# A gated linear recurrence with an erf network behind it, on one core: weights narrowed by an integer addition, checks moved from the scalar to the vector engine

## The chip, the cores and the metric

The kernel runs on one core of one Trainium2 chip. A core has a matrix engine (PE, which loads weights as PEld and multiplies), a vector engine (DVE), a scalar engine (ACT), GpSimd (POOL), and queues that start transfers (DMA; SP is the engine that issues most of them). Each engine works through its own list of instructions in order; semaphores hold one until another has done its part. The metric is the time of one execution on the device, in microseconds (us). Here the median of the runs is 747.3 us.

## The reference

Two blocks follow each other. The first is a recurrence with a complex gate: for every batch, head and step t, a state S of 48 x 48 is turned and shrunk by the gate a, takes up the outer product of k and v, and is read by q. The second is a dense network with two weight matrices.

```python
# batch 4, heads 8, steps 768, head dim 48; tokens 3072, model 384, hidden 2048
mag = sqrt(a_re**2 + a_im**2)
scale = minimum(mag, 0.999) / (mag + 1e-6)
a_re_n, a_im_n = a_re * scale, a_im * scale
for t in range(S):
    S_re, S_im = ar*S_re - ai*S_im + outer(k[t], v[t]), ar*S_im + ai*S_re
    y[t] = q[t] @ S_re
# x: (tokens, 384), the heads side by side
h = x @ w_in                                   # 384 -> 2048
sp = maximum(h, 0) + log1p(exp(-abs(h)))       # softplus
out = (h * erf(sp)) @ w_out                    # 2048 -> 384
```

q, k, v and the gates are 4-byte floats. The weights arrive as 8-byte floats, 12.6 MB of them, and the kernel has to make 4-byte floats of them itself.

## The kernel before

The tokens are worked off in 12 units of 256 (`u`), each of two chunks of 128 (`c`). For each chunk the gates give an angle (arctan of a_im / a_re, summed over time by a product with a triangle of ones) and a decay (logarithms, summed likewise). Keys and queries are scaled and turned by them (`prep`), transposed by PE (`cols`), multiplied with each other (`scores`), and give the chunk's output `y` and the state for the next chunk (`state`). Then `ff_in` multiplies with w_in, `softplus` and `erf_times_h` apply the nonlinearity, and `ff_out` multiplies with w_out. A table of places, `WHEN`, says when each step is put among the others.

This way of computing is only right if the gates and weights lie in certain ranges, for instance |a_im| < a_re. So the kernel collects measures of them in the tiles `seen` while it runs, and at its end compares them with limits; if one is out of range, a slower path recomputes everything. The parts that the change touches are these.

Narrowing. The 8 bytes of a weight are two words, `lo` and `hi`. The weights come in 16 pieces of 128 x 768, eight of w_in (128 x 3 x 256) and eight of w_out:

```python
def seek(words, i):                       # how many weights are too close to zero
    hi = words.bitcast(FP)...[:, :, 1]
    act(out=hi, in_=hi, func=AF.Square)
    act(out=hi, in_=hi, func=AF.Exp, scale=-1e10, accum_out=zeros[:, i:i + 1])

def begin():
    ...
    ins = nc.scalar.mul(out=b, in_=lo, mul=2.0**-52)                              # ACT
    nc.vector.tensor_scalar(out=a, in0=hi, 0x07FFFFFF, 3, and, shift_left)        # DVE
    nc.vector.scalar_tensor_tensor(out=u, in0=hi, 0xC0000000, in1=a, and, or)     # DVE, into the weights
    nc.vector.tensor_scalar(out=a, in0=u, scalar1=0xFF800000, and)                # DVE, sign and exponent alone

def end():
    f, b, a = T["parts", i]
    nc.vector.tensor_tensor(out=b, in0=b, in1=a, op=OP.mult)                      # DVE
    nc.vector.tensor_tensor(out=f, in0=f, in1=b, op=OP.add)                       # DVE

# each piece: get (transfer), use (begin and end), again (a second transfer, later), look (seek on it)
```

(The arguments are shortened here.) The high word is cut to a 4-byte float with the last three bits of its mantissa at zero, and the low word is added as a float of the right size. The second transfer of each piece, between the fifth and the last unit, serves the check alone; the last two pieces are looked at in halves, so there are 18 looks.

Gates, per unit or, in the first two units, per chunk:

```python
def g_mag(u, cc=ALL):
    act(out=s, in_=ar, func=AF.Square, accum_out=large[:, i:i + 1])
    act(out=y, in_=ai, func=AF.Square)
    nc.vector.tensor_tensor(out=s, in0=s, in1=y, op=OP.add)

def g_off(u, cc=ALL):                     # is |a_im| < a_re everywhere?
    act(out=m, in_=ai, func=AF.Abs)
    nc.vector.tensor_tensor(out=m, in0=m, in1=ar, op=OP.subtract)
    act(out=m, in_=m, func=AF.Relu, bias=LEAST, accum_out=off[:, i:i + 1])

def g_tan(u, cc=ALL):
    act(out=th, in_=ar, func=AF.Ln)
    act(out=th, in_=th, func=AF.Exp, scale=-1.0)
    nc.vector.tensor_tensor(out=th, in0=th, in1=ai, op=OP.mult)     # a_im / a_re
```

The first steps of the program. `warm` issues products that nothing reads:

```python
WARM = (12, 9, 8, 4, 6)
def warm(n, t):
    for _ in range(n):
        tc.keep_in_program_order(nc.tensor.matmul(out=ps[:, 0:P], lhsT=t[:, 0:P], rhs=t[:, 0:P], start=True, stop=True))
...
warm(WARM[0], cold)
...
for c in range(C):
    g_tan(0, one[c]); g_mag(0, one[c]); warm(WARM[1 + c], T["th", 0][:, c])
... # logarithms, arctan, angle and decay of the first chunk
warm(WARM[3], T["th", 0][:, 1])
g_sin(0, c0)
for f in first[:2]: f()                   # prep of k and q, first chunk
g_angle(0, 1)
warm(WARM[4], T["th", 0][:, 1])
g_sin(0, c1)
...
for cc in one: g_off(0, cc)
```

A transposed query tile is copied out of PSUM by ACT in the first units (`u < WHEN["qact"]`, which is 3), later by DVE.

Of the kernel before, what the change touches and what calls it, by code (L numbers as in the profile page):

```python
# [10 lines left out]
FP = mybir.dt.float32  # L11
U8 = mybir.dt.uint8
I32 = mybir.dt.int32
U32 = mybir.dt.uint32
# [15 lines left out]

LEAST = 2.0**-30

# [4 lines left out]
def weave(*streams):  # L37
# [5 lines left out]
    for _, _, _, step in sorted(order, key=lambda e: e[:3]):  # L43
# [3 lines left out]

WHEN = {'qact': 3,
 'a00': [0.385, 0.377, 0.405, 0.415, 0.427, 0.308, 0.569, 0.485, 0.567, 0.63],
 'a01': [0.562, 0.528, 0.613, 0.636, 0.651, 0.625, 0.661, 0.663, 0.673, 0.683],  # L50
 'n': [0.676, 0.782, 0.769, 0.929, 1.105, 1.183, 1.312, 1.472, 1.61, 1.914, 1.96, 2.143, 2.151, 2.284, 2.395],
 'g1': [0.657, 0.707, 0.747, 0.758, 0.79, 0.797, 0.829],
 'att': {1: [[0.95, 1.297], 1.089], 2: [[1.716, 2.126], 1.029], 3: [[3.038, 3.627], 1.205]},
 'gate': {2: [1.242, 1.292, 1.402, 1.421, 1.352, 1.472, 1.392], 3: [1.516, 1.614, 1.92, 2.114, 2.598, 2.232, 2.18]},
 'hps': {0: [[0.75, 0.876], [1.01, 1.45]],
         1: [[1.788, 2.0], [2.366, 2.708]],
         2: [[3.136, 3.566], [3.538, 3.85]],
         11: [[11.947, 12.305], [12.367, 12.72]]},
 'act': {0: [2.6, 2.924],
         1: [3.335, 3.7],  # L60
         2: [4.208, 4.46],
         3: [4.9, 5.2],
         4: [5.752, 6.098],
         10: [11.62, 11.97],
         11: [12.455, 12.8]},
 'ops': {0: [3.02, 3.377, 3.703],
         1: [3.679, 4.329, 4.479],
         2: [4.454, 4.8, 4.886],
         3: [5.38, 5.6, 6.213],
         10: [12.123, 12.388, 12.988],  # L70
         11: [13.11, 13.3, 14.0]},
 'T': 5.1,
 'gr': [-1.569, -1.419, -1.119, -0.953, -0.498, -0.129, -1.299],
 'st': [0.014, 0.03, 0.059, 0.09, 0.12, 0.15, 0.2, 0.25, 0.28, 0.388],
 'hr': [1.117, 1.488, 1.588, 1.938],
 'ar': [1.565, 1.95],
 'or': [2.163, 2.683, 3.173],
 'c1': 0.5,
 'er': 0.25,
 'ag': [5.424, 6.26, 7.239, 8.239, 9.239, 10.239, 11.21],  # L80
 'n1': 2,
 'rest': 12.3,
 'ok': 13.7,
 'al': [[11.0, 11.39], [11.319, 11.75]]}


WARM = (12, 9, 8, 4, 6)

# [510 lines left out]
def quotient_path(  # L599
# [74 lines left out]
    spans, off, large, exps, inverse, zeros = seen  # L674
    for t in (off, large, zeros):
        nc.vector.memset(t, 0.0)

# [69 lines left out]
    def narrow(i, dst, src, home):  # L747
# [6 lines left out]
        def seek(words, i):  # L754
            hi = words.bitcast(FP).rearrange("p (n w) -> p n w", w=2)[:, :, 1]
            act(out=hi, in_=hi, func=AF.Square)
            act(out=hi, in_=hi, func=AF.Exp, scale=-1e10, accum_out=zeros[:, i:i + 1])

# [6 lines left out]
        def begin():  # L765
            words = T["raw", i].bitcast(U32).rearrange("p (k n w) -> p k n w", k=k_, w=2)
            lo, hi = words[..., 0], words[..., 1]
            f, u = dst, dst.bitcast(U32)
            a, b = split(sp.tile([P, PARTS], U32, tag="S", name="word")[:, 0:N]), lo.bitcast(FP)
            ins = nc.scalar.mul(out=b, in_=lo, mul=2.0**-52)  # L770
            if i < 3:
                in_order(ins)
            ins = nc.vector.tensor_scalar(out=a, in0=hi, scalar1=0x07FFFFFF, scalar2=3, op0=OP.bitwise_and,
                                          op1=OP.logical_shift_left)
            if "hold" in T:
                tc.add_manual_dep(ins.ins, T["hold"].ins.name, order, reason="place among others")
            nc.vector.scalar_tensor_tensor(out=u, in0=hi, scalar=0xC0000000, in1=a, op0=OP.bitwise_and,
                                           op1=OP.bitwise_or)
            nc.vector.tensor_scalar(out=a, in0=u, scalar1=0xFF800000, scalar2=None, op0=OP.bitwise_and)
            T["parts", i] = f, b, a.bitcast(FP)  # L780

        def end():
            f, b, a = T["parts", i]
            nc.vector.tensor_tensor(out=b, in0=b, in1=a, op=OP.mult)
            nc.vector.tensor_tensor(out=f, in0=f, in1=b, op=OP.add)  # L785

# [76 lines left out]
    def gate(u, cc):  # L863
        return [T[nm, u][:, cc[0]:cc[1]].rearrange("p c h d -> p c (h d)") for nm in ("ar", "ai")]
# [10 lines left out]

    def g_off(u, cc=ALL):

        ar, ai = gate(u, cc)
        m = T["y"][:, cc[0]:cc[1]]
        i = u * C + cc[0]  # L880
        act(out=m, in_=ai, func=AF.Abs)
        nc.vector.tensor_tensor(out=m, in0=m, in1=ar, op=OP.subtract)
        act(out=m, in_=m, func=AF.Relu, bias=LEAST, accum_out=off[:, i:i + 1])

    def g_tan(u, cc=ALL):
        ar, ai = gate(u, cc)
        th = g_("th", u, cc)
        act(out=th, in_=ar, func=AF.Ln)
        act(out=th, in_=th, func=AF.Exp, scale=-1.0)
        nc.vector.tensor_tensor(out=th, in0=th, in1=ai, op=OP.mult)  # L890

    def g_log(u, cc=ALL):
# [70 lines left out]
    def chunk(u, c):  # L963
# [14 lines left out]
        def cols(nm, g):  # L978
            def f():
                ps = ps_a.tile([P, HG, P], FP, tag="a", name="tr")  # L980
                for j in range(HG):
                    nc.tensor.transpose(out=ps[0:D2, j, :], in_=st[nm][:, g * HG + j].rearrange("p u d -> p (u d)"),  # L982
                                        identity=ident)
                t = att2.tile([P, HG, P], FP, tag=f"{nm}T", name=f"{nm}T", bufs=2 if nm == "k" else 3)
                (nc.scalar.copy if nm == "k" or u < WHEN["qact"] else nc.vector.tensor_copy)(out=t[0:D2], in_=ps[0:D2])  # L985
                st[nm, g] = t
            return f
# [283 lines left out]
    g_decay(0, 1)  # L1271
    for cc in one:
        g_off(0, cc)

    plan = list(zip(WHEN["a00"][2:], first[2:])) + list(zip(WHEN["a01"], chunk(0, 1)))
    plan += [(0.60, partial(load_qkv, 1))] + [(0.605, wt[j][0]) for j in (6, 7)]
    plan += [(WHEN["n"][j - 1], wt[j][1]) for j in range(2, 16)]
# [9 lines left out]
    for c, b in enumerate((E0, E1)):  # L1287
        plan += [(b, partial(f, 1, one[c])) for f in (g_tan, g_mag, g_log, g_off)] + [(b + 0.03, partial(g_total, 1, c))]
    plan += [(dec, partial(g_decay, 1, c)) for c in range(C)] + [(S1 + 0.001, partial(load_gates, 2))]
# [4 lines left out]
    for u in range(NU):  # L1294
# [5 lines left out]
        if u > 1:  # L1300
            mag, log, turn, angle, decay, sin, get = WHEN["gate"].get(
                u, [u + x for x in WHEN["gr"]])
            plan += [(mag, partial(g_mag, u)), (mag, partial(g_off, u)), (log, partial(g_tan, u)), (log, partial(g_log, u))]
            plan += [(turn, partial(g_turn, u)), (sin, partial(g_sin, u))]
# [12 lines left out]
    def check():  # L1317

        n = len(seen)
        sums = const.tile([P, n], FP, name="sums")  # L1320
        for i, t in enumerate(seen):
            nc.vector.tensor_reduce(out=sums[:, i:i + 1], in_=t, axis=mybir.AxisListType.X, op=OP.add)
# [63 lines left out]
```

## Time and profile before

| | |
|---|---|
| median of the runs | 747.3 us (746.47 to 753.23) |
| span of the profiled execution | 749.0 us |
| mean granted clock of PE | 0.978 |
| bytes moved | 54.5 MB, mean 73 GB/s |
| chain of work that ended last | PE 45%, ACT 28%, DVE 18%, DMA 5%, no visible wait 2% |

The page has the busy time of each engine, then the span in 40 slices of 18.7 us, in which a digit is the busy share in tenths and PEclk the clock that PE was granted. A product in 4-byte floats stands as two records. The groups name the line, engine, operation, tiles and shape, then busy time and the mean of one instruction, then the idle time of its engine just before and what ended that. The records of matrix products overlap each other, so their mean says less than the distance from one to the next: eight products of the second network, 16 records, take 5.16 us back to back.

### The profile page before, as it was taken

Reading aid. Unit: us, or ns where it says so; the run is one execution under the profiler, and the core shown is the slowest. Engines: PE = TensorE matmul, PEld = TensorE weight load, DVE = VectorE, ACT = ScalarE, POOL = GpSimd, SP = SyncE. Lnnn points to the kernel's source line nnn. Section 1 sums busy time; section 2 is a strip of 40 time slices with the busy share of each in tenths; the row PEclk is TensorE's granted clock in tenths of the full one; section 3 lists DMA queues with packets and bytes.
Section 4 is the critical chain, followed back from the end, with each engine's and each line's share of the span. In section 5 each row is a group of like instructions: output and inputs, shape, how many; then the busy total and the mean of one; then the engine's idle time right before and its main releaser. Section 6 shows DMA issues by size and latency. Waiting matters only on the chain.

```text
span 749.0 us, 12674 instructions
## 1 busy us (share of the span) xinstructions
PE 715.4 (96%) x5018; PEld 608.9 (81%) x5018; DVE 586.0 (78%) x1011; ACT 618.4 (83%) x849; POOL 1.1 (0%) x8
## 2 busy tenths in 40 slices
PE   8898989989999999999999999999999999999996
PEld 6677778866677678898898899898889889899985
DVE  6779999597858698969959949949949957956663
ACT  8797685997989998999798798798798788697760
POOL 0000000000000000000000000000000000000000
PEclk9599899999999999999999999999999999999999
DMA  9963666311212030350530521522311410300000
GB/s 222 226 145 61 158 162 166 67 28 26 44 33 47 27 54 22 59 134 22 138 51 25 137 43 35 137 37 60 111 33 49 96 33 22 127 1 16 7 22 26
DMA packets 156012, 54.50 MB, mean 73 GB/s; under 512 B 142612, under 2 KB 145704, under 8 KB 155944
## 3 DMA queue, kind: packets, MB, share of 16 engines
q1 hardware_dynamic: 153864, 53.22, 30.4%
q8 instruction: 41, 0.67, 0.4%
q10 hardware_dynamic: 2080, 0.39, 0.3%
q14 instruction: 27, 0.22, 0.1%
HBM read 48.82 MB, written 4.75 MB: 72 GB/s over the span
## 4 chain that ended last, share of the span: by engine, by line
PE 45%; ACT 28%; DVE 18%; DMA 5%; issue 2%; SPq 0%; DVEq 0%
PE hps L1062 16%; PE ops L1160 8%; PE ops L1122 6%; ACT L707 5%; ACT z L708 5%; ACT yy L708 4%; PE y L1042 4%; PE kv L1005 3%; DVE z L1090 3%; DVE yy L1091 3%; PE sc L993 3%; DVE e L1092 3%; PE tr L982 3%; ACT e L708 2%; DVE h L1093 2%
## 5 line engine op out<-in xcount | busy, mean ns | idle before, releaser
L1062 PE MATMUL hps<-xT,w_in_sb 128*128 128x256 f32 x1152 | 273.6, 384 | 5.7 <-DVE w_in_sb L785 4.6
L1062 PEld LDWEIGHTS hps<-xT,w_in_sb 128*128 128x128 f32 x1152 | 214.1, 191 | 40.7 <-issue 4.7
L707 ACT ACT_TABLE_LOAD x77 | 98.8, 1283 | 3.3 <-issue 2.1
L1090 DVE TENSOR_TENSOR z<-z,yy 128x512 f32<-128x512 f32 x96 | 62.5, 683 | 34.5 <-ACT e L708 34.3
L708 ACT ACTIVATE e<-z 128x512 f32<-128x512 f32 x96 | 57.3, 626 | 31.8 <-DVE h L1093 31.4
L1122 PE MATMUL ops<-w_out_sb,h 128*128 128x384 f32 x224 | 78.9, 498 | 1.0 <-DVE h L1093 1.0
L1064 ACT COPY h<-hps 128x512 f32<-128x512 f32 x96 | 55.0, 576 | 27.2 <-PE hps L1062 27.1
L1160 PE MATMUL ops<-w_out_sb,h 128*128 128x192 f32 x384 | 70.1, 326 | 1.0 <-DVE o L1171 1.0
L1160 PEld LDWEIGHTS ops<-w_out_sb,h 128*128 128x128 f32 x384 | 63.6, 190 | 2.4 <-DVE o L1171 1.4
L1122 PEld LDWEIGHTS ops<-w_out_sb,h 128*128 128x128 f32 x224 | 42.3, 194 | 27.1 <-issue 1.9
L1091 DVE SCALAR_TENSOR_TENSOR yy<-z,yy 128x512 f32<-128x512 f32 x96 | 62.4, 682 | 0.2
L1092 DVE TENSOR_TENSOR e<-e,yy 128x512 f32<-128x512 f32 x96 | 62.4, 682 | 0.1
L1093 DVE SCALAR_TENSOR_TENSOR h<-e,h 128x512 f32<-128x512 f32 x96 | 62.4, 682 | 0.1
L993 PE MATMUL sc<-qT,kT 96*128 96x128 f32 x384 | 52.5, 286 | 0.2 <-DVE qT L985 0.2
L993 PEld LDWEIGHTS sc<-qT,kT 96*128 96x128 f32 x384 | 49.4, 199 | 3.0 <-DVE qT L985 0.9
L1042 PE MATMUL y<-A,v 128*32 128x128 f32 x768 | 48.3, 281 | 1.9 <-ACT pr L708 1.1
L708 ACT ACTIVATE z<-h 128x2048 f32<-128x2048 f32 x24 | 45.9, 1911 | 4.3 <-DVE yy L1091 4.2
L1160 PE MATMUL ops<-T,S 128*128 128x192 f32 x256 | 48.0, 331 | 0.0
L708 ACT ACTIVATE yy<-z 128x2048 f32<-128x2048 f32 x24 | 45.9, 1912 | 0.4
L708 ACT ACTIVATE z<-z 128x2048 f32<-128x2048 f32 x24 | 45.9, 1913 | 0.3
L708 ACT ACTIVATE yy<-yy 128x2048 f32<-128x2048 f32 x24 | 45.9, 1911 | 0.3
L1160 PEld LDWEIGHTS ops<-T,S 128*128 128x128 f32 x256 | 43.2, 194 | 2.3 <-DVE S L1107 0.2
(107 smaller groups left out, 1128.9 us busy)
## 6 DMA issues: line engine op xcount, KB each, us to landing
raw<-in_moe_w_in_dram SPq DMA_DIRECT2D x8, 768.0 KB
raw<-in_moe_w_out_dram SPq DMA_DIRECT2D x8, 768.0 KB, 4.2
again<-in_moe_w_in_dram SPq DMA_DIRECT2D x8, 768.0 KB, 4.8
ar<-in_a_re_dram SPq DMA_DIRECT2D x24, 192.0 KB, 3.1
k<-in_k_dram SPq DMA_DIRECT2D x24, 192.0 KB, 4.0
q<-in_q_dram SPq DMA_DIRECT2D x24, 192.0 KB, 3.7
v<-in_v_dram SPq DMA_DIRECT2D x48, 96.0 KB, 3.3
out_dram<-o SPq DMA_DIRECT2D x24, 192.0 KB, 1.9
```

The costliest lines, as they stand in the source:

```text
L707: in_order(nc.scalar.preload_act_table_set(sets[0]))
L708: in_order(nc.scalar.activation(func=func, **kw))
L993: nc.tensor.matmul(out=ps[:, j, :], lhsT=st["k", g][0:D2, j, :], rhs=st["q", g][0:D2, j, :], start=True, stop=True)
L1042: nc.tensor.matmul(out=ps[b * QUAD:(b + 1) * QUAD, i, :], lhsT=lhsT, rhs=rhs, start=start, stop=stop)
L1062: nc.tensor.matmul(out=ps[:, e, :], lhsT=w_in_sb[:, kd, f0:f0 + P], rhs=T["xT", u][:, kd, :], start=(kd == 0), stop=(kd == KD - 1))
L1064: nc.scalar.copy(out=T["h", u, sl][:, i:i + 2, :], in_=ps)
L1090: nc.vector.tensor_tensor(out=z, in0=z, in1=y, op=OP.mult)
L1091: nc.vector.scalar_tensor_tensor(out=y, in0=z, scalar=-2.0, in1=y, op0=OP.add, op1=OP.mult)
L1092: nc.vector.tensor_tensor(out=e, in0=e, in1=y, op=OP.mult)
L1093: nc.vector.scalar_tensor_tensor(out=h, in0=e, scalar=1.0 / RT2, in1=h, op0=OP.add, op1=OP.mult)
L1122: nc.tensor.matmul(out=ps, lhsT=lhsT, rhs=w_out_sb[:, i, :], start=i == HALF, stop=i == KF - 1)
L1160: ins = nc.tensor.matmul(out=ps, lhsT=a(sl)[:, i], rhs=b(sl, i), start=sl == 0 and i == 0, stop=sl == NSL - 1 and i == HALF - 1)
```

## The change

It has five parts. A weight is narrowed by adding integers: ACT makes of the low word its upper three bits, rounded, and DVE adds them to the cut high word, so that a carry runs from the mantissa into the exponent by itself; this spares the mask and the multiplication. The checks of weights and angles are done by single reductions of DVE (the least absolute high word; the greatest absolute a_im / a_re) in place of chains on ACT. More unread products are issued at first. The query copies of the third unit move from ACT to DVE. And the places were fitted anew. What it is for: less work on ACT and DVE, and a PE that is not left idle in the first steps.

The core of the diff; most changed places in `WHEN` are cut:

```diff
-WARM = (12, 9, 8, 4, 6)
+WARM = (12, 9, 8, 8, 13, 5)
-WHEN = {'qact': 3,
+WHEN = {'qact': 2,
... (places of steps changed: some by a few hundredths of a unit; 'al', the last looks, by 0.15)
+ 'qone': 0}

         def seek(words, i):
             hi = words.bitcast(FP).rearrange("p (n w) -> p n w", w=2)[:, :, 1]
-            act(out=hi, in_=hi, func=AF.Square)
-            act(out=hi, in_=hi, func=AF.Exp, scale=-1e10, accum_out=zeros[:, i:i + 1])
+            nc.vector.tensor_reduce(out=zeros[:, i:i + 1], in_=hi, axis=mybir.AxisListType.X, op=OP.min,
+                                    apply_absolute_value=True)
...
-            ins = nc.scalar.mul(out=b, in_=lo, mul=2.0**-52)
+            ins = nc.scalar.mul(out=lo, in_=lo, mul=2.0**-29)
...
-            nc.vector.scalar_tensor_tensor(out=u, in0=hi, scalar=0xC0000000, in1=a, op0=OP.bitwise_and,
+            nc.vector.scalar_tensor_tensor(out=a, in0=hi, scalar=0xC0000000, in1=a, op0=OP.bitwise_and,
                                            op1=OP.bitwise_or)
-            nc.vector.tensor_scalar(out=a, in0=u, scalar1=0xFF800000, scalar2=None, op0=OP.bitwise_and)
...
         def end():
-            f, b, a = T["parts", i]
-            nc.vector.tensor_tensor(out=b, in0=b, in1=a, op=OP.mult)
-            nc.vector.tensor_tensor(out=f, in0=f, in1=b, op=OP.add)
+            a, lo = T["parts", i]
+            nc.vector.tensor_tensor(out=dst.bitcast(U32), in0=a, in1=lo, op=OP.add)
...
-    def g_off(u, cc=ALL):
-        ... (the three steps above)
     def g_tan(u, cc=ALL):
...
         nc.vector.tensor_tensor(out=th, in0=th, in1=ai, op=OP.mult)
+        i = u * C + cc[0]
+        nc.vector.tensor_reduce(out=off[:, i:i + 1], in_=th, axis=mybir.AxisListType.XY, op=OP.max,
+                                apply_absolute_value=True)
...
+    plan += [(0.40, partial(warm, WARM[5], T["th", 0][:, 1]))]
...
     def check():
+        nc.vector.tensor_scalar(out=off, in0=off, scalar1=-1.0, scalar2=0.0, op0=OP.add, op1=OP.max)
+        nc.vector.tensor_scalar(out=zeros, in0=zeros, scalar1=4e-5, scalar2=None, op0=OP.is_lt)
```

## The prediction

> **What bounds the kernel now.** I read the page's busy shares and slices first, then the windows view over stretches of 20 us and over single steps of the clock, then what PE waited for, and last the groups of the operations that the change touches. The share of busy time would end the matter at once:
>
> ```profile
> PE 715.4 (96%) x5018; PEld 608.9 (81%) x5018; DVE 586.0 (78%) x1011; ACT 618.4 (83%) x849; POOL 1.1 (0%) x8
> PE   8898989989999999999999999999999999999996
> PEclk9599899999999999999999999999999999999999
> ```
>
> With PE at 96% an engine that sheds other work seems to win nothing. But the clock's second slice is a 5, so part of PE's busy time is slow work. The windows view (time, then busy us of PE, PEld, DVE, ACT, POOL, then clock, DMA share, GB/s) shows where:
>
> ```profile
> 20.00:40.00 20.00, 17.86 (x117) 14.47 (x118) 14.15 (x23) 14.86 (x32) 0.00 (x0) 0.58 0.93 219
> 40.00:60.00 20.00, 18.38 (x135) 14.00 (x134) 17.31 (x32) 16.84 (x38) 0.00 (x0) 1.00 0.58 134
> 60.00:80.00 20.00, 16.33 (x90) 14.02 (x89) 19.90 (x29) 14.25 (x24) 0.00 (x0) 0.86 0.33 81
> 80.00:100.00 20.00, 17.99 (x203) 14.35 (x201) 17.75 (x30) 14.57 (x25) 0.00 (x0) 0.97 0.52 129
> 100.00:120.00 20.00, 18.94 (x162) 16.52 (x162) 18.35 (x30) 14.31 (x21) 0.00 (x0) 1.00 0.80 195
> 120.00:140.00 20.00, 20.00 (x159) 16.55 (x155) 18.97 (x28) 16.43 (x26) 0.00 (x0) 1.00 0.57 140
> 200.00:300.00 100.00, 99.11 (x610) 73.11 (x611) 78.56 (x137) 90.86 (x108) 0.00 (x0) 0.98 0.19 38
> ```
>
> From 200 us on PE is the bound: 0.9 us idle in 100. The first 140 us are another kernel: from 60 to 140 us DVE is busy 75 of 80 us, and PE idles 6.7 us and runs slow besides. A finer cut shows how the clock falls:
>
> ```profile
> 16.30:19.75 3.45, 1.43 (x13) 1.24 (x11) 3.00 (x5) 3.44 (x8) 0.00 (x0) 1.00 0.93 245
> 26.60:30.00 3.40, 3.40 (x20) 3.15 (x19) 0.21 (x1) 3.09 (x9) 0.00 (x0) 0.50 0.73 143
> 71.00:74.40 3.40, 1.03 (x10) 0.83 (x8) 3.40 (x5) 1.98 (x3) 0.00 (x0) 0.99 1.02 189
> 77.80:81.20 3.40, 3.40 (x9) 2.70 (x8) 3.40 (x6) 1.33 (x4) 0.00 (x0) 0.50 0.77 223
> ```
>
> Twice a stretch in which PE did 1.4 or 1.0 of 3.4 us is followed by half clock: from 19.75 to 36.8 us, and from 74.4 to 81.2 us. What PE waited for in those places, with total, times and longest:
>
> ```profile
> PE hps L1062 <- DVE w_in_sb L785: 4.6, 2, 3.5
> ...
> PE tr L982 <- DVE qt L974: 2.2, 1, 2.2
> PE tr L982 <- ACT qT L985: 2.0, 1, 2.0
> ```
>
> The 3.5 us wait is the one before 75.5 us, for a narrowed weight piece; the other two lie at 17.7 and 21.9 us.
>
> **What the Trainium skill says.** "TensorE: Matmul & The Clock Gate", section "What's actually happening": the slow clock is the default, a busy window of about 3.4 us releases it and an idle one brings it back. The trace agrees on the step (3.4 us) and the halving; it adds that a stretch 58% idle (16.30 to 19.75) is idle enough, and that coming back took 17 us the first time and 6.8 the second. "DVE: scalar operands, raw-bit mode, write accounting and state across instructions", section "Raw-bit mode": the DVE's adder is exact on bit patterns only below 2^24. So a 32-bit sum has to be made of halves; in the changed program's order of instructions the add does stand with elements of half a word (512 where the tile has 256). No run here has its time yet. "VectorE: DVE Perf Modes", section "The perf-mode tier table": tensor_reduce has only the 1x program. The one here is too small to tell (128x24 in 169 ns), so I price it as the 1x tensor_tensor of the same size.
>
> **The change part by part.** The groups (count, busy us, mean ns, idle before):
>
> ```profile
> L784 DVE TENSOR_TENSOR raw<-raw,word 128x768 f32<-128x768 f32 x16 | 15.3, 955 | 3.8 <-ACT raw L770 3.5
> L785 DVE TENSOR_TENSOR w_in_sb<-w_in_sb,raw 128x768 f32<-128x768 f32 x8 | 7.6, 949 | 0.0
> L779 DVE TENSOR_SCALAR word<-w_in_sb 128x768 uint32<-128x768 uint32 x8 | 7.6, 946 | 0.1
> L779 DVE TENSOR_SCALAR word<-w_out_sb 128x768 uint32<-128x768 uint32 x8 | 4.4, 555 | 0.1
> L703 ACT ACTIVATE again<-again 128x768 f32<-128x768 f32 x14 | 12.9, 920 | 5.1 <-DMA again<-in_moe_w_out_dram 4.2 <-DMA again<-in_moe_w_in_dram 0.9
> ```
>
> Narrowing, 16 pieces. L779 and L784 go, and L785 becomes the integer add. Removed: 0.95 + 0.95 = 1.90 us for each of 8 w_in pieces, 0.55 + 0.95 = 1.51 us for each of 8 w_out pieces, together 27.3 us. The add: if it takes a word in a cycle as L785 does, 0.95 us; I put 1.05 us, an estimate from that row with 0.1 us for being a program of its own, so 16 x 0.1 = 1.6 us come back. DVE: -25.7 us, all of it in the first 140 us, where DVE is the full engine.
>
> Checks of the weights. ACT loses 14 x (920 + 914) ns + 4 x (557 + 579) ns + 18 x 189 ns for reading the accumulator = 33.6 us, all after 300 us. DVE gains 14 x 0.95 + 4 x 0.56 = 15.5 us there, at 75 to 82% busy.
>
> Checks of the angles. For ten whole units ACT loses 842 + 838 + 191 ns, for four half ones 514 + 516 + 191 ns: 23.6 us. DVE loses one subtraction each (948 or 556 ns) and gains one reduction that I price the same: nothing.
>
> Query copies of unit 2 go from ACT to DVE (4 x 575 ns off ACT, 4 x 679 ns on to DVE). Unread products: 4 to 8, 6 to 13, and 5 new. At full clock 34 of their records took 4.18 us and a product has two, so one takes 0.25 us and 16 more take 3.9 us, laid into the idle stretches at 13.6, 17.7 and 21.9 us.
>
> Totals: ACT 618 to about 559 us, DVE 586 to about 578 us, PE the same work. Now to the path, stage by stage.
>
> 1. 17 to 40 us: 13 products fill some 2.9 us from 16.2 us on, so the stretch before 19.75 is no longer idle and the clock should stay up. From 26.6 to 33.4 us PE alone sets the pace (DVE is busy 0.21 us in one of those steps): its kv and score products take 6.2 us at half clock and would take 3.1. Transposes and the first y products (about 6 us of path in this stage) give another 2 us, and the first query copy, which now stands before two ACT steps (1.0 us) and after a removed Abs (0.5 us), gives 1 us. Sum -6 us.
> 2. 53 to 140 us: DVE sheds 13 pieces: 5 x 1.8 + 8 x 1.41 = 20 us. PE cannot follow all the way: its idle time there is 1.6 (50 to 60) + 3.7 + 2.0 + 1.1 = 8.4 us, and the second half-clock stretch costs half of 5.7 busy us = 2.8 us. Of these 11.2 us I take three quarters: -8.5 us.
> 3. 140 to 200 us: PE idles 3.5 us, ACT is at 91% and loses about 6 us of angle checks and copies: -1 us.
> 4. 200 to 730 us: PE idles 8.2 us and two short clock drops cost 3.4 us; some of that is ACT standing at the second load of weights (7.0 us of waits), but DVE will stand there now: -1.5 us.
> 5. Unread products that get in the way +1 us, two more small DVE steps in the closing check (137 to 169 ns each) +0.2 us.
>
> Sum: -6 - 8.5 - 1 - 1.5 + 1.2 = -15.8 us. 747.3 - 15.8 = 731.5 us, 2.1% less.
>
> **The rivals.** (a) PE is the bound and the shed work lay beside it. For: 96%, and 0.9 us idle per 100 after 200 us. Against: the slow clock and the waits at the start. It would give 743 to 747 us. (b) The integer add runs half a word per cycle: about 1.75 us, an estimate from twice L785's time less its start. Then DVE sheds 14.5 us instead of 25.7, stage 2 halves and the time is some 737 us. (c) The clock falls anyway, a step later (an idle stretch at 22 or 30 us): stage 1 gives 2 instead of 6, some 735 us. (d) DVE, now with the checks, stands before a late load and holds what PE wants after 400 us. Against: DVE is idle there a fifth of the time. It would add 3 to 5 us. (e) The relieved ACT (59 us) tightens stages 3 and 4 fully: down to 723 us.
>
> **Range and chances.** (a) to (d) are each less likely than not and mostly add, (e) stands against them; I take 723 to 741 us. The border of 2% is 732.4 us, just above my figure. Places that were fitted to this kernel speak for the gain to be realised; so faster by over 2% 0.55, within 2% 0.44, slower by over 2% 0.01.
>
> **What would show it.** Right: no half clock between 19.75 and 37 us nor near 75 us; the first hps product, at 45.2 us now, 5 to 8 us earlier; the wait of hps for w_in_sb below 1 us; the integer add at 1.0 to 1.2 us; the last narrowed piece, at 139.6 us now, before 125 us; ACT near 559 us and DVE near 578 us; from 200 us to the end nearly the same length. Wrong: a half-clock stretch of more than one step before 100 us, an add above 1.5 us, or more PE idle time after 300 us, behind DVE's reductions of the weights.

## The result and the profile after

The changed kernel takes 723.11 us in the median (722.15 to 725.71, 4 runs), the kernel before 748.12 us beside it (746.47 to 753.23): a ratio of 0.966, 95% interval 0.9605 to 0.9715. The profiled execution went from 749.0 to 720.6 us. The gain is 25 us, more than half as much again as the 15.8 us worked out. 723.1 us lies at the fast end of the stated 723 to 741 us; by the ratio, 747.3 x 0.966, it is 721.9 us, just beyond that end. The direction was right; two terms of the sum were too small.

The page after, busy shares first, then slices of 18 us:

```profile
PE 703.3 (98%) x5050; PEld 601.6 (83%) x5050; DVE 577.6 (80%) x1003; ACT 568.1 (79%) x749; POOL 1.1 (0%) x8
PE   8899999999999999999999999999999999999996
PEclk9999999999999999999999999999999999999999
```

ACT has shed 50 us (to 568; 559 us were predicted), DVE 8 us (578 predicted). The durations of ACT's records do sum to 59 us less, as worked out; but neighbouring records overlap, by some 0.09 us in the lines shown under e15, and busy time counts an overlap once, so 100 instructions fewer take 8 us of overlap with them. PE's busy time fell by 12 us though it does 16 more products: it has less slow time. The 5 in the clock's row is gone. The windows view of the changed kernel, the same stretches by the clock on the wall as were shown of the kernel before:

```profile
20.00:40.00 20.00, 18.72 (x209) 15.39 (x210) 16.52 (x32) 18.04 (x40) 0.00 (x0) 1.00 0.93 216
40.00:60.00 20.00, 19.88 (x106) 16.35 (x106) 12.97 (x22) 15.29 (x28) 0.00 (x0) 1.00 0.60 140
60.00:80.00 20.00, 20.00 (x172) 16.73 (x171) 19.55 (x30) 19.31 (x29) 0.00 (x0) 1.00 0.83 193
80.00:100.00 20.00, 18.81 (x179) 16.82 (x178) 19.71 (x33) 15.49 (x23) 0.00 (x0) 1.00 0.74 187
100.00:120.00 20.00, 20.00 (x202) 16.47 (x195) 16.22 (x24) 13.68 (x20) 0.00 (x0) 1.00 0.63 150
200.00:300.00 100.00, 99.53 (x645) 75.69 (x644) 90.42 (x157) 90.97 (x115) 0.00 (x0) 1.00 0.22 44
```

From 40 to 120 us PE is idle for 1.3 us in all. From 60 to 100 us DVE is as full as before (39.3 and 37.7 of 40 us), but with more of the work done by then. The groups of the changed operations (count, busy us, mean ns, idle before):

```profile
L782 DVE CUSTOM_DVE_ANT_0 w_in_sb<-raw,word 128x1536 uint16<-128x1536 uint16 x8 | 7.7, 958 | 5.7 <-PE hps L1053 4.2 <-ACT raw L769 1.4
L756 DVE TENSOR_REDUCE seen<-again 128x1 f32<-128x768 f32 x14 | 13.1, 945 | 2.7 <-DMA again<-in_moe_w_out_dram 1.8 <-DMA again<-in_moe_w_in_dram 0.7
L880 DVE TENSOR_REDUCE seen<-th 128x1 f32<-128x768 f32 x10 | 9.5, 949 | 0.1
```

The add costs 0.96 us where 1.05 us were put in, and it now waits for PE (4.2 us) where PE waited for it before. The reductions cost what the prediction took. All PE waits of one us or more that are left in the whole run:

```profile
PE tr L973 <- DVE kt L965: 2.1, 5, 0.9
PE sc L984 <- DVE qT L976: 1.3, 1, 1.3
PE tr L973 <- ACT kT L976: 1.3, 3, 0.8
PE unread L1210 <- DVE cold L665: 1.1, 1, 1.1
```

The wait of hps for w_in_sb, 4.6 us before, is gone. Of the other signs, these came true: the first hps product at 40.0 us instead of 45.2, the last narrowed piece at 116.8 us, no half clock before the closing steps. ACT's 559 us and the equal length from 200 us on did not.

**Where the time came from.** A stretch of the clock on the wall holds different work in the two kernels, so I lined them up by work. Each product that is read was given the distance at which products of its kind follow each other back to back; this sums to 663.5 us in every kernel here. A mark is the moment in the trace at which so much of this work is done.

| mark (us of work) | before | after | lead gained in the stage | predicted |
|---|---|---|---|---|
| 15 | 43.3 | 37.4 | -5.9 (stage 1) | -6 |
| 90 | 136.0 | 118.3 | -11.8 (stage 2) | -8.5 |
| 140 | 190.3 | 171.6 | -1.0 (stage 3) | -1 |
| 658 | 736.7 | 709.1 | -8.9 (stage 4) | -1.5 |
| end of the span | 749.0 | 720.6 | -0.8 (closing) | +1.2 |

The stages sum to the 28.4 us between the two spans, 3 us more than between the medians: the profiled execution of the kernel before took 750.8 us in all, 2.7 us above its median. The last stage can be read directly, since both windows hold the same 518 us of work. Before:

```profile
190.30:736.70 546.40, 537.03 (x3827) 468.62 (x3826) 429.82 (x750) 465.65 (x605) 0.00 (x0) 0.99 0.24 55
```

After:

```profile
171.60:709.10 537.50, 533.30 (x3830) 465.98 (x3829) 444.20 (x771) 423.57 (x528) 0.00 (x0) 1.00 0.24 57
```

PE's idle time fell from 9.4 to 4.2 us, and its busy time by 3.7 us with the same products, which is about half of the 6.8 us of half clock that only the kernel before had there. ACT went from 85% of the stretch to 79%, DVE from 79% to 83%.

### The profile page after: what moved, and what is told of

Its sections match the earlier page's. It is cut to its first block, busy times and chain, and to the rows that moved or that the text cites. A ratio compares the mean times of both kernels' runs of the same rounds, so it can differ in the third digit from the quotient of the medians.

```text
span 720.6 us, 12616 instructions
## 1 busy us (share of the span) xinstructions
PE 703.3 (98%) x5050; PEld 601.6 (83%) x5050; DVE 577.6 (80%) x1003; ACT 568.1 (79%) x749; POOL 1.1 (0%) x8
## 4 chain that ended last, share of the span: by engine, by line
PE 49%; ACT 25%; DVE 18%; DMA 5%; issue 3%; SPq 0%; ACTq 0%; DVEq 0%
PE hps L1053 19%; PE ops L1151 12%; ACT z L708 5%; ACT yy L708 5%; ACT L707 5%; PE sc L984 3%; PE y L1033 3%; PE tr L973 3%; DVE z L1081 3%; DVE yy L1082 3%; DVE e L1083 3%; PE kv L996 2%; DVE h L1084 2%; PE ops L1113 2%; DMA again<-in_moe_w_out_dram 2%
## 5 line engine op out<-in xcount | busy, mean ns | idle before, releaser
L1053 PE MATMUL hps<-xT,w_in_sb 128*128 128x256 f32 x1152 | 270.8, 381 | 1.3 <-ACT xT L1037 0.7
L708 ACT ACTIVATE e<-z 128x512 f32<-128x512 f32 x96 | 57.3, 626 | 37.2 <-DVE h L1084 36.8
L1113 PE MATMUL ops<-w_out_sb,h 128*128 128x384 f32 x224 | 76.6, 488 | 0.4 <-DVE h L1084 0.4
L984 PEld LDWEIGHTS sc<-qT,kT 96*128 96x128 f32 x384 | 47.9, 192 | 5.7 <-DVE qT L976 3.0
L984 PE MATMUL sc<-qT,kT 96*128 96x128 f32 x384 | 51.0, 278 | 1.7 <-DVE qT L976 1.3
```

What stands on the lines that cost most here:

```text
L708: in_order(nc.scalar.activation(func=func, **kw))
L984: nc.tensor.matmul(out=ps[:, j, :], lhsT=st["k", g][0:D2, j, :], rhs=st["q", g][0:D2, j, :], start=True, stop=True)
L1053: nc.tensor.matmul(out=ps[:, e, :], lhsT=w_in_sb[:, kd, f0:f0 + P], rhs=T["xT", u][:, kd, :], start=(kd == 0), stop=(kd == KD - 1))
L1113: nc.tensor.matmul(out=ps, lhsT=lhsT, rhs=w_out_sb[:, i, :], start=i == HALF, stop=i == KF - 1)
```

## The experiments

The change was taken apart into five parts: A, the check of the angles on DVE; L, the looks at the weights on DVE; N, the narrowing by an integer addition; U, the unread products; P, the places with the query copies of the third unit. Some kernels take one part out of the changed kernel, others put one or two into the kernel before. "Front" is the mark at 140 us of work, "late" the time from there to 658; both are of the one profiled execution. The median and the clock (mean granted clock of PE over a run, again the median) are of all runs; the clock of the kernel before is that of the 136 runs made beside the experiments.

| kernel | parts | median us | ratio to before, 95% | clock | front | late |
|---|---|---|---|---|---|---|
| before | none | 748.12 | 1 | 0.985 | 190.3 | 546.4 |
| e6 | N | 745.85 | 0.9971 (0.9948 to 0.9995) | 0.984 | 183.5 | 552.9 |
| e7 | U | 745.95 | 0.9964 (0.9941 to 0.9988) | 0.990 | 190.0 | 543.9 |
| e9 | P | 746.69 | 0.9997 (0.9971 to 1.0022) | 0.987 | 182.2 | 549.7 |
| e14 | N, P | 743.31 | 0.9949 (0.9918 to 0.9979) | 0.987 | 182.3 | 550.8 |
| e15 | A in the first two units | 744.51 | 0.9943 (0.9920 to 0.9965) | 0.983 | 182.8 | 546.5 |
| e16 | A in the other ten units | 745.42 | 0.9954 (0.9933 to 0.9975) | 0.987 | 189.0 | 542.4 |
| e10 | A | 738.87 | 0.9894 (0.9860 to 0.9928) | 0.992 | 185.9 | 542.2 |
| e11 | L | 744.31 | 0.9935 (0.9918 to 0.9953) | 0.986 | 190.6 | 540.4 |
| e12 | N, L | 741.47 | 0.9921 (0.9898 to 0.9945) | 0.986 | 189.5 | 542.6 |
| e13 | N, A | 736.94 | 0.9842 (0.9804 to 0.9880) | 0.992 | 178.5 | 545.1 |
| e17 | A, P | 735.23 | 0.9839 (0.9791 to 0.9886) | 0.995 | 177.8 | 542.3 |
| e4 | all but A | 738.01 | 0.9839 (0.9782 to 0.9896) | 0.990 | 181.4 | 542.1 |
| e3 | all but L | 728.54 | 0.9718 (0.9668 to 0.9769) | 0.998 | 171.6 | 543.5 |
| e8 | A, L | 736.49 | 0.9857 (0.9793 to 0.9921) | 0.988 | 183.0 | 537.1 |
| e5 | all but P | 730.49 | 0.9771 (0.9722 to 0.9821) | 0.998 | 176.8 | 539.8 |
| e2 | all but N | 728.76 | 0.9711 (0.9660 to 0.9761) | 0.998 | 179.4 | 536.5 |
| e1 | all but U | 725.40 | 0.9670 (0.9622 to 0.9718) | 0.993 | 174.0 | 539.5 |
| after | all | 723.11 | 0.9660 (0.9605 to 0.9715) | 0.998 | 171.6 | 537.5 |

The last column sorts itself largely by one thing: how many checks ACT still has in the later units. Two (the first six rows; e15 keeps both there): 543.9 to 552.9 us. One: 540.4 to 545.1. None: 536.5 to 539.8. Narrowing, places and unread products are in kernels of each kind and don't break this order, though the first two kinds overlap by a microsecond.

One profiled execution can lie away from its median: those of e6, e12, e14 and e10 are 4.8, 4.0, 3.1 and 2.7 us above theirs, that of e8 is 2.3 us below, so two or three us between two fronts or two late stages say little. Much of the spread is the clock: the 136 runs of the kernel before have clocks of 0.976 to 0.990 and times of 743.9 to 757.1 us, and a straight line through them gives 6.5 us for 0.01. At that rate the change's rise from 0.985 to 0.998 is worth some 8 of its 25 us, an estimate. Taken out of the changed kernel, only A (0.990) and U (0.993) let the clock fall; N, L and P leave it at 0.998.

### One part taken out of the changed kernel

**e1: the old numbers of unread products.**

```diff
-WARM = (12, 9, 8, 8, 13, 5)
+WARM = (12, 9, 8, 4, 6, 0)
```

> The changed kernel (723.1 us) with the old numbers of unread products, 4, 6 and none in place of 8, 13 and 5. Theory (they keep the clock up): a half-clock stretch of some 17 us comes back at about 20 us and the time is 728 to 731 us. Rival (the clock stays up because the relieved DVE and ACT feed PE sooner): no half clock in the first 100 us, 722 to 725 us.

725.40 us, 2.3 us more than the changed kernel; the ranges of the two overlap (724.91 to 726.91 here). The clock falls again, from 21.1 to 27.9 us and from 181.5 to 188.3 us, but for 6.8 us each. At 15 us of work the kernel is 1.4 us behind, and the clock of its runs is 0.993 instead of 0.998. The unread products do what they are for, but with the rest of the change in place it is worth little. Neither theory fits.

**e2: the old narrowing.**

```diff
-            ins = nc.scalar.mul(out=lo, in_=lo, mul=2.0**-29)
+            ins = nc.scalar.mul(out=b, in_=lo, mul=2.0**-52)
...
+            nc.vector.tensor_scalar(out=a, in0=u, scalar1=0xFF800000, scalar2=None, op0=OP.bitwise_and)
...
-            nc.vector.tensor_tensor(out=dst.bitcast(U32), in0=a, in1=lo, op=OP.add)
+            nc.vector.tensor_tensor(out=b, in0=b, in1=a, op=OP.mult)
+            nc.vector.tensor_tensor(out=f, in0=f, in1=b, op=OP.add)
```

> The changed kernel with the narrowing of before: DVE gets back two operations for each of 16 pieces, some 27 us, in the first 120 us. Theory (DVE is the bound of that stretch): the last piece lands 12 us later or more, the time is 732 to 737 us. Rival (other parts of the change had already freed DVE): below 727 us.

728.76 us, between the theories: the narrowing is worth 5.7 us in the median and 7.8 us at the front mark. The last piece is narrowed 18.6 us later. The loss lies wholly in front, as predicted, but is only part of the front's gain.

**e3: the looks back on ACT.**

```diff
-            nc.vector.tensor_reduce(out=zeros[:, i:i + 1], in_=hi, axis=mybir.AxisListType.X, op=OP.min,
-                                    apply_absolute_value=True)
+            act(out=hi, in_=hi, func=AF.Square)
+            act(out=hi, in_=hi, func=AF.Exp, scale=-1e10, accum_out=zeros[:, i:i + 1])
```

> The changed kernel with the check of the weights back on ACT: 33 us of ACT more after 300 us, 15 us of DVE less. Theory (the 10 us won after 140 us come from the relief of ACT): 727 to 731 us, with PE waiting for ACT's decay or copies again. Rival (they come from the new places): 722 to 725 us.

728.54 us, as the theory had it; the front is the same to a tenth of a microsecond, and the late stage 6.0 us longer. Here are the PE waits of e3 from 300 to 712 us:

```profile
PE kv L996 <- ACT pr L708: 2.6, 4, 1.1
PE tr L973 <- ACT kT L976: 1.7, 3, 0.9
PE ops L1151 <- DVE o L1162: 1.7, 1, 1.7
PE tr L973 <- DVE kt L965: 1.0, 1, 1.0
```

In the changed kernel the same view has two lines:

```profile
PE tr L973 <- DVE kt L965: 1.2, 4, 0.5
PE tr L973 <- ACT kT L976: 0.2, 1, 0.2
```

The looks themselves never appear as what PE waits for. What appears is `pr` and `kT`, short steps that come after a look in ACT's list: a look of two passes, with its wait for the second transfer (6.9 us of such waits in e3, 7.0 in the kernel before), holds them up. The kernel before shows the whole of it in the chain of work that ended last (start, length, what):

```profile
538.23 6.35 DMA again<-in_moe_w_out_dram
544.58 0.02 issue
544.60 0.91 ACT again L703
545.51 0.46 ACT h L1064
545.97 0.89 ACT again L708 x2
546.86 0.85 ACT pr L708 x3
547.71 0.04 issue
547.76 1.89 PE kv L1005 x16
```

The second transfer lands, the two passes of the look follow, then `pr`, and then the `kv` products, for which PE had stood idle for 1.2 us. In e3 all four waits for `pr` have a look just ahead in the same way. On DVE the same look holds up nothing that PE needs at once: ACT itself waits 4.9 us for looks in the changed kernel, and PE doesn't wait behind it. Of the 6.0 us that e3 loses late, 5.5 are idle time of PE. This is most of the missing late gain of 7.4 us (8.9 measured, 1.5 predicted).

**e4: the check of the angles back on ACT.**

```diff
+        act(out=m, in_=ai, func=AF.Abs)
+        nc.vector.tensor_tensor(out=m, in0=m, in1=ar, op=OP.subtract)
+        act(out=m, in_=m, func=AF.Relu, bias=LEAST, accum_out=off[:, i:i + 1])
...
-        nc.vector.tensor_reduce(out=off[:, i:i + 1], in_=th, axis=mybir.AxisListType.XY, op=OP.max,
-                                apply_absolute_value=True)
```

> The changed kernel with the check of the angles back on ACT as Abs, subtraction, Relu: 24 us of ACT more over the whole span, DVE the same. Theory (ACT's relief): 726 to 730 us, some 2 us of it in the first 60 us. Rival (the new places): 722 to 725 us.

738.01 us: 15 us more (13 by the ratios), beyond both theories, and the costliest part to lose. It is 9.8 us behind at the front mark and 4.6 us longer late. In its first 60 us the PE waits begin with

```profile
PE sum L915 <- ACT th L709: 3.2, 2, 2.9
PE tr L980 <- ACT qT L983: 1.8, 1, 1.8
```

Neither wait is there with more than 0.5 us in the changed kernel. (In this profiled execution a load of a_im for the first unit also landed 1.6 us late and put back all that follows; that much is not the edit's.)

**e5: the old places,** with the query copies of the third unit left on DVE.

```diff
- 'a01': [0.526, 0.422, 0.611, ...],
+ 'a01': [0.562, 0.528, 0.613, ...],
... (all other entries of WHEN likewise)
```

> The changed kernel with all places of before (the query copies of unit 2 stay on DVE). Theory (the moved and saved work makes the gain, the places only trim it): 727 to 733 us. Rival (most of the gain is the fitting): above 736 us.

730.49 us, as the theory had it: 5.2 us at the front mark, 2.3 us late.

### Parts put into the kernel before

**e6: N alone** (the lines of e2 the other way round).

```diff
-            nc.vector.tensor_tensor(out=b, in0=b, in1=a, op=OP.mult)
-            nc.vector.tensor_tensor(out=f, in0=f, in1=b, op=OP.add)
+            nc.vector.tensor_tensor(out=dst.bitcast(U32), in0=a, in1=lo, op=OP.add)
```

> The kernel before with the narrowing by an integer addition alone. Theory (DVE is the bound from 53 to 140 us and sheds 26 us): 736 to 741 us, the last piece at 128 us or earlier, no half clock near 75 us. Rival (PE cannot follow, or another wait takes over): above 744 us.

745.85 us (740.38 to 751.25, 20 runs), in the rival's range. Of the theory the last piece (at 125.5 us) and the missing half clock near 75 us came true, but not the time. At the front mark the kernel is 6.8 us ahead, close to the predicted 8.5, though part of that is the clock's (6.8 us of half clock there, 23.9 in the kernel before). Its late stage is 6.5 us longer:

```profile
183.50:736.40 552.90, 542.25 (x3828) 473.23 (x3827) 430.80 (x751) 466.40 (x606) 0.00 (x0) 0.98 0.23 55
```

PE is idle 10.7 us there (9.4 before), and its clock is halved for 17.0 us, at 191.2, 542.8, 600.8 and 652.0 us (6.8 us before, at 200.7 and 548.8). The Trainium skill, "TensorE: Matmul & The Clock Gate", section "HAM oscillation — how this bites in real kernels", prices such a stretch at half its length. That makes 8.5 against 3.4 us, an estimate, 5.1 more; the trace agrees with 5.2 more busy us for the same products. With 1.3 us of idle time this is the whole loss in this execution. But this execution took 750.67 us, 4.8 above the median, and the clock of all 20 runs, 0.984, is that of the kernel before: narrowing alone leaves the amount of half clock as it was. The PE waits from 150 us on begin with

```profile
PE kv L1002 <- ACT pr L708: 3.7, 5, 1.5
PE tr L979 <- ACT kT L982: 2.5, 3, 1.9
```

**e7: U alone.**

```diff
-WARM = (12, 9, 8, 4, 6)
+WARM = (12, 9, 8, 8, 13, 5)
+    plan += [(0.40, partial(warm, WARM[5], T["th", 0][:, 1]))]
```

> The kernel before with the new unread products alone (8, 13 and 5). Theory (they hold the clock up in the first 37 us): no half clock from 19.75 to 36.8 us, 742 to 745 us. Rival (the idle time near 30 us lets it fall anyway): 746 to 749 us.

745.95 us, between the two ranges. In the profiled execution the rival was right: the clock is halved from 25.3 to 39.0 us instead of 19.8 to 36.8. But the clock of that execution is 0.984. The median of the 20 runs is 0.990, and nine of them lie above 0.990, which none of the 136 runs of the kernel before does. So the unread products hold the clock up in part of the runs, and the gain of 0.36% fits that.

**e8: A and L together, all else old.**

```diff
-            act(out=hi, in_=hi, func=AF.Square)
-            act(out=hi, in_=hi, func=AF.Exp, scale=-1e10, accum_out=zeros[:, i:i + 1])
+            nc.vector.tensor_reduce(out=zeros[:, i:i + 1], in_=hi, ..., op=OP.min, apply_absolute_value=True)
...
-    def g_off(u, cc=ALL):
+        nc.vector.tensor_reduce(out=off[:, i:i + 1], in_=th, ..., op=OP.max, apply_absolute_value=True)
```

> The kernel before with both checks, of the weights and of the angles, on DVE; nothing else is changed. Theory (ACT's relief is worth 10 us after 140 us and some at the start): 735 to 740 us. Rival (without fitted places the relief lies beside the path): 744 to 748 us.

736.49 us: the two checks alone bring nearly half of the gain. In the profiled execution the late stage has the whole of its gain already, 537.1 us against 537.5 in the changed kernel:

```profile
183.00:720.10 537.10, 534.64 (x3828) 466.50 (x3827) 441.96 (x767) 422.80 (x525) 0.00 (x0) 1.00 0.24 56
```

**e9: P alone.**

```diff
-WHEN = {'qact': 3,
- 'a01': [0.562, 0.528, 0.613, ...],
+WHEN = {'qact': 2,
+ 'a01': [0.526, 0.422, 0.611, ...],
```

> The kernel before with nothing but the new places (and the query copies of unit 2 on DVE). Theory (the places are fitted to the shed work and are worth something only with it): 744 to 750 us, with the half clock before 37 us still there. Rival (the places are worth some 7 us by themselves, as they are when they are taken out of the changed kernel): 738 to 743 us.

746.69 us, no difference that can be measured, as the theory had it. Its profiled execution is ahead in front (with 6.8 us of half clock there) and longer late, like e6's.

**e10: A alone** (the angle lines of e8).

```diff
-    def g_off(u, cc=ALL):
+        nc.vector.tensor_reduce(out=off[:, i:i + 1], in_=th, ..., op=OP.max, apply_absolute_value=True)
```

> The kernel before with only the check of the angles moved to DVE. Theory (this check stood in the chain of the first units, where ACT's absolute value and relu sat before the steps that PE waits for, and it is the larger of the two checks): 738 to 742 us, ahead of before by 4 us or more when PE has done 60 us of its products. Rival (the two checks together give their 12 us only because ACT is relieved as a whole, each alone little): 743 to 747 us.

738.87 us, as the theory had it, the largest single part.

**e11: L alone** (the weight lines of e8).

```diff
-            act(out=hi, in_=hi, func=AF.Square)
-            act(out=hi, in_=hi, func=AF.Exp, scale=-1e10, accum_out=zeros[:, i:i + 1])
+            nc.vector.tensor_reduce(out=zeros[:, i:i + 1], in_=hi, ..., op=OP.min, apply_absolute_value=True)
```

> The kernel before with only the check of the weights moved to DVE. Theory (worth what taking it out of the changed kernel cost, some 4 to 5 us, all after 300 us, as PE no longer stands behind ACT's pr and kT): 742 to 745 us, no difference before 300 us. Rival (the place of the look matters little as long as ACT has the angles too): 746 to 749 us.

744.31 us, as the theory had it; the front is unchanged (190.6 us) and the late stage 6.0 us shorter, the same 6.0 that e3 lost.

**e12: N and L.**

```diff
+            nc.vector.tensor_reduce(out=zeros[:, i:i + 1], in_=hi, ..., op=OP.min, apply_absolute_value=True)
...
+            nc.vector.tensor_tensor(out=dst.bitcast(U32), in0=a, in1=lo, op=OP.add)
```

> The kernel before with the narrowing by an integer addition and the check of the weights on DVE, the rest as before. With the narrowing alone 8 us were gained in the first 100 us of products and lost again, most of it after 500 us. Theory (it is ACT, with its looks at the weights, that gives it back late): the gain is kept, 735 to 740 us. Rival (it is given back by the clock or by the places, whatever ACT does): 741 to 746 us.

741.47 us, inside the rival's range: 0.8% where N and L alone sum to 0.9%. So relieving ACT of the looks does not by itself keep the narrowing's lead. Its profiled execution, 4.0 us above the median of the 11 runs, drew the long stretch of half clock, 17.1 us from 23.6 us on, so that its front is no measure of the narrowing.

**e13: N and A.**

```diff
+        nc.vector.tensor_reduce(out=off[:, i:i + 1], in_=th, ..., op=OP.max, apply_absolute_value=True)
...
+            nc.vector.tensor_tensor(out=dst.bitcast(U32), in0=a, in1=lo, op=OP.add)
```

> The kernel before with the narrowing by an integer addition and the check of the angles on DVE, the rest as before. The narrowing alone gave 2 us, the angles alone 9. Theory (the lead of the narrowing is lost because PE runs up against ACT; with ACT relieved in every unit the lead is kept): 730 to 734 us. Rival (the two simply add, as narrowing and the check of the weights did): 735 to 739 us.

736.94 us, the rival's range: 1.6%, with 1.35% the sum of the two alone. The front's lead is 11.8 us, and from 28 us until the closing steps the clock doesn't fall.

**e14: N and P.**

```diff
-WHEN = {'qact': 3,
+WHEN = {'qact': 2,
...
+            nc.vector.tensor_tensor(out=dst.bitcast(U32), in0=a, in1=lo, op=OP.add)
```

> The kernel before with the narrowing by an integer addition and the new places, both checks still on ACT. Each alone gave 2 us or less. Theory (the places are fitted to the earlier weights and keep the lead): 735 to 740 us. Rival (with ACT loaded as before the lead goes, whatever the places): 742 to 747 us.

743.31 us, the rival's range. In the profiled execution the front is 8.0 us ahead and the late stage 4.4 us longer than before: with both checks on ACT half of that lead goes in spite of the new places.

**e15: A in the first two units alone.**

```diff
     def g_tan(u, cc=ALL):
+        if u < 2:
+            nc.vector.tensor_reduce(out=off[:, i:i + 1], in_=th, ..., op=OP.max, apply_absolute_value=True)
...
-    for cc in one:
-        g_off(0, cc)
```

> The kernel before with the check of the angles moved to DVE for the first two units alone (four half-unit checks, 4.9 us off ACT). Theory (what the check of the angles was worth is mostly its place in the chain of the first units): 741 to 744 us, the lead there by 60 us of products and constant after. Rival (it is ACT's load over the whole run): 745.5 to 748 us.

744.51 us. By work its lead is 7.5 us at the front mark (with 10.2 us of half clock there, 23.9 before, so that some of it is the clock's; over its 20 runs the clock, 0.983, is no better than that of the kernel before, so the median's 0.57% owe it nothing) and nothing more comes later (546.5 us, as before). The theory's shape holds, its range is missed by half a microsecond. What the check did there can be seen in ACT's timeline (start, length, instruction) of the kernel before:

```profile
21.89 0.52 ACT L708 ACTIVATE s<-s 128x384 f32<-128x384 f32 x1
22.32 0.51 ACT L703 ACTIVATE y<-y 128x384 f32<-128x384 f32 x1
22.73 0.19 ACT L703 ACTIVATION_READ_ACCUMULATOR y<-y 128x1 f32 x1
22.82 0.51 ACT L708 ACTIVATE y<-s 128x384 f32<-128x384 f32 x1
23.24 0.56 ACT L985 COPY qT<-tr 96x512 f32<-96x512 f32 x1
```

and of e15:

```profile
20.35 1.28 ACT L708 ACT_TABLE_LOAD   x1
21.64 0.52 ACT L709 ACTIVATE s<-s 128x384 f32<-128x384 f32 x1
22.07 0.56 ACT L990 COPY qT<-tr 96x512 f32<-96x512 f32 x1
```

The relu of the check (`y<-y`) and the reading of its sum stood before the query copy for which PE's transposes waited 2.0 us. Without them the copy comes 1.2 us earlier, and the transposes behind it with it, at 22.69 instead of 23.85 us (0.25 us of that from the absolute value, further ahead in the list; the rest from the relu and from one logarithm step that now stands after the copy).

**e16: A in the other ten units alone.**

```diff
     def g_tan(u, cc=ALL):
+        if u >= 2:
+            nc.vector.tensor_reduce(out=off[:, i:i + 1], in_=th, ..., op=OP.max, apply_absolute_value=True)
...
-            plan += [(mag, partial(g_mag, u)), (mag, partial(g_off, u)), ...]
+            plan += [(mag, partial(g_mag, u)), ...]
```

> The kernel before with the check of the angles moved to DVE for the ten later units alone (18.7 us off ACT). Theory (mostly the first units): 743 to 747 us. Rival (ACT's load over the whole run): 739 to 742 us, the lead growing from 150 us on.

745.42 us, in the theory's range, but the two halves weigh nearly the same: 0.57% and 0.46% sum to the 1.06% of e10. The check acted in both places, in the first units and in the other ten. Whether it is ACT's load there or the place of single steps in its list, these two runs don't separate.

**e17: A and P.**

```diff
-WHEN = {'qact': 3,
+WHEN = {'qact': 2,
...
+        nc.vector.tensor_reduce(out=off[:, i:i + 1], in_=th, ..., op=OP.max, apply_absolute_value=True)
```

> The kernel before with the check of the angles on DVE and the new places; the narrowing, the check of the weights and the unread products as before. The places alone gave nothing, the angles alone 8 us; taken out of the changed kernel the places cost 8 and the angles 13. Theory (the places were fitted to steps without the check of the angles and pay as soon as that is off ACT): 730 to 735 us. Rival (the places pay only when the weights come early too): 737 to 740 us.

735.23 us, at the border of the theory's range. With the angles off ACT the places are worth 4 us (e10 to e17), alone nothing (e9), in the changed kernel 7 (e5). So they are worth more with the angles off ACT; which part brings the rest is not shown (with the narrowing alone, e14, they are worth 0.2%, inside the intervals).

**The parts together.** Alone they bring 1.06% (A), 0.65% (L), 0.36% (U), 0.29% (N) and 0.03% (P), a sum of 2.4%; the change brings 3.4%. Half of the missing percent is the pair of A and P: together they bring 1.6% (e17), 0.5% more than the two alone, though that is no more than the width of e17's interval to either side. Taken out one at a time the parts cost 1.8 (A), 1.1 (P), 0.6 (L), 0.5 (N) and 0.1 (U) percentage points, 4.1 in sum. So the parts help each other: they bring less alone than together and cost more when they leave.

## Why the prediction was wrong

- **Stage 1, -6 us predicted, -5.9 measured: the number held, its reason in part.** I laid five of the six to the clock, kept up by unread products. Taken out of the changed kernel they cost 1.4 us at the first mark (e1); alone they hold the clock up in some runs (e7). The clock itself is worth less than I thought: e11 and e16 have the same work in front as the kernel before, and drew 6.8 us of half clock where it drew 17.1; they reach the first mark at 42.4 and 41.2 us, 0.9 and 2.1 us earlier. The angle check before the first copies is worth about as much: with the same 6.8 us of half clock e15 is 2.3 us ahead of e16. The narrowing, of which my sum for this stage has nothing, is worth 1.3 us (e2). That the sum came out is luck.
- **Stage 2, "Of these 11.2 us I take three quarters: -8.5 us": too small.** Measured is -11.8, about the whole of PE's idle and slow time there (idle 8.3 to 1.3 us, busy 4.8 us less). And the step gave it all to DVE's relief. Narrowing taken out costs 7.8 us at the front mark (e2), the angles 9.8 (e4, up to 1.6 of them its late load), the places 5.2 (e5): in sum more than the 18.7 us gained there. Put in alone they bring 6.8, 4.4 and 8.1 (e6, e10, e9), so single executions don't settle the shares. In e4 PE waits for ACT's `th` and `qT`: ACT, and not DVE alone, sets the pace of the front.
- **The cost of the angle check, "nothing", was the price on DVE.** That price was right (0.95 us for 0.95 us). Of its 23.6 us on ACT I counted half a microsecond before the first copy (stage 1) and part of the 1 us of stage 3, and nothing after 200 us. It is the largest part: 1.06% alone, 1.8% when taken out.
- **Stage 3, -1 us: right** (-1.0).
- **Stage 4, "some of that is ACT standing at the second load of weights ... but DVE will stand there now: -1.5 us": this step failed most.** Measured is -8.9 us, of 13.1 us that were there to be had (9.4 idle and 3.7 slow): 7.4 of the 12.6 us that the sum fell short of the two profiled spans. I took the wait for the second load as costing PE the same behind either engine. DVE does stand there now, for 2.5 us, but PE does not stand behind it. On ACT the look stood ahead of `pr` and `kT`; put back there it costs 6.0 us late (e3). The angles put back cost another 4.6 (e4), which this step didn't count either. "From 200 us to the end nearly the same length" was wrong with it.
- **Stage 5, +1.2 us: no sign of it.** The stretch after the last mark is 0.8 us shorter.
- **Rivals.** (e), the relieved ACT tightens stages 3 and 4 fully, down to 723 us, came nearest: stage 4 did, stage 3 hardly (1.0 us). I let it stand for the lower end of the range only. (b) fell with the add's 0.96 us, (a) with the table, (d) with the PE waits. Of the profiled kernels with the new unread products only e7 drew (c).

Why the narrowing's lead is lost when it comes alone stays open. The arithmetic of e6 shows where it goes in one execution, into half clock and idle time, with ACT's `pr` and `kT` as what PE waits for. But over all runs the clock is the same with and without the narrowing (0.984 and 0.985): where a run has its half clock, in front or late, may be chance, and part of the lead with it. That relief of ACT keeps the lead is not shown: with the angles off ACT (e13) the narrowing is worth 0.5%, with the looks off (e12) 0.1%, alone 0.3%, with intervals of 0.2 to 0.4 to either side.

## What to carry to other kernels

When an engine that is not the bound sheds work, don't price the work by its share of busy time: look in its list for short steps that the bound engine waits for, and see what stands ahead of them. A long step with a wait of its own, ahead of such a step, can hold PE up wherever PE has caught up (0.4 to 1.1 us at a time behind the looks of e3), so put it on the engine whose next steps are not urgent. Fitted places brought nothing alone and 7 us with the rest, so test them with the work that they were fitted to. And before a stage of one profiled execution is explained, compare its time and clock with those of the other runs.

## What the runs showed of the hardware

- The integer addition of 768 words per partition stands in the trace as a custom program on 1536 halves and takes 957 ns in the mean of both weights, as long as a float `TENSOR_TENSOR` of 768 words (955 ns). At this size the halves cost no time.
- The smallest absolute value of every second word (945 ns) costs the same as the largest of packed words (949 ns).
- Before the closing steps half clock came in pieces of 3.4, 6.8, 13.7 and 17.1 us, and its first stretch was 6.8 us in e11 and e16 and 17.1 us in the kernel before, with the same work in front.
- Over 136 runs of one kernel 0.01 less mean clock, which is 15 us of half clock, went with 6.5 us more time.
